# Two matmuls instead of three for a split product, with the correction sums in columns of their own

## The chip, the cores and the metric

The kernel runs on one core of a Trainium2 chip. The metric is the device time of one execution in microseconds. TensorE multiplies, VectorE and ScalarE work element by element and can read the accumulators (PSUM), GpSimd works on SBUF only, and SyncE sends most of the DMAs.

## The reference

Three stages, float32. A landmark attention (4 batches, 8 heads, 576 tokens, 64 per head, 32 landmarks) gives x of 2304 x 512. A first MLP follows, and then a second one, in which the change lies:

```
h = x @ w_in2                      # 2304 x 512 @ 512 x 2048
g = h * clip(h + 3, 0, 6) / 6
out = g @ w_out2                   # 2304 x 2048 @ 2048 x 512
```

## The kernel before

**Split numbers.** Float32 matrices are multiplied in a faster format (F32R) by splitting each operand into a high and a low part: `high = round(x)`, `low = x - high`. A product is then three passes, high x high, high x low and low x high (`PASSES`, line 21; the helper `passes`, line 132). The helper `split` (line 126) makes the parts of a tile: ScalarE casts the high one (line 128), VectorE subtracts to get the low one (line 129).

**Second MLP.** The 2304 tokens are worked off in three blocks of 768 (`i` = 0, 1, 2). In each block the first product of the MLP (`unit1`, eight units) fills `g`, 2048 x 768, in SBUF, and then the second (`product2`) multiplies it with w_out2. Both use a Strassen-like form with 7 products of quarter matrices instead of 8. The seven of the second product are called in the order `ORDER` = 0, 1, 6, 5, 4, 2, 3. Each takes a left factor of 384 tokens and a right factor of 256 columns and sums over `NU` = 8 steps `kp` of 128.

**One step** of `product2`: for four of the seven products VectorE first combines two quarters of `g` in place (lines 1021 to 1027, 128x384). `split` then makes the high and low part `s` of the left factor, 128x384 each, in a ring of 11 buffers, so that the splits can run that many steps ahead of TensorE. The right factors have been split long before and come from device memory as weight tiles `st` of 1 MB, half a product each, in six buffers. For each of `NQ` = 3 thirds `t` of 128 tokens TensorE does the three passes: a weight load (128 columns of `s`) and a matmul that moves 256 columns of `w`. The layout of `w` for one step is two column halves `j`, each with its high and low part `z` of 128 columns.

**Sums.** The three thirds accumulate in two PSUM banks of 512 columns, `qa` (thirds 0 and 1) and `qb` (third 2), from the pool `ps_o` of four banks, so that one product is summed while another is read. The pool `ps_h` (two banks) is used by `unit1` alone. After a product `evacuated` reads the sums: product 0 through ScalarE into `u2` (line 1048), the others through VectorE, which adds the running sums `u2`, `u3` (line 1050). Four of the seven products end in `stored`: the result goes to a tile `ob` and by a DMA of SyncE to the output (line 1058). Products 5 and 4 of the form are evacuated twice.

**Order of the work.** TensorE's and SyncE's instructions stand in the order in which the program writes them (`manual_schedule`); a planner with estimated durations orders those of VectorE, ScalarE and GpSimd and fills their gaps with later work. During a block's second product VectorE and ScalarE also make the next block's forms `yf` (`forms_y`, lines 917 and 129), from `yr`, which SyncE loads at the start of the block (`load_y`, line 905), behind the last output of the block before.

**GpSimd** has additions in `unit1` (lines 999 and 1002, 128x384) and, in the stages before, in the preparation of the weights (line 852, 128x128); in `product2` it has none.

Of the kernel before, what the change touches and what calls it, by code (L numbers as in the profile page):

```python
# [10 lines left out]
F32 = mybir.dt.float32  # L11
# [4 lines left out]
AF = mybir.ActivationFunctionType  # L16
ALU = mybir.AluOpType
# [3 lines left out]
PASSES = ((0, 0), (0, 1), (1, 0))  # L21
# [43 lines left out]
def kernel(  # L65
# [24 lines left out]
    nc = tc.nc  # L90
# [3 lines left out]
    P = 128  # L94
# [11 lines left out]
    scale = 1.0 / float(D) ** 0.5  # L106
# [16 lines left out]
    def pool(name, bufs=1, st=ctx, **kw):  # L123
        return st.enter_context(tc.tile_pool(name=name, bufs=bufs, reuse_waits="tile", **kw))

    def split(hi, lo, src, rest=nc.vector):
        return (
            nc.scalar.copy(hi, src),  # L128
            rest.tensor_tensor(out=lo, in0=src, in1=hi.bitcast(F32), op=ALU.subtract),  # L129
        )  # L130

    def passes(ps, lhs, rhs, first=True, last=True, **kw):
        for i, (x, y) in enumerate(PASSES):
            nc.tensor.matmul(ps, lhsT=lhs(x), rhs=rhs(y), start=first and i == 0, stop=last and i == 2, **kw)  # L134
# [27 lines left out]
    NU = NK // 2  # L162
# [548 lines left out]
    first = (mybir.EngineType.PE, mybir.EngineType.DVE, mybir.EngineType.Activation, mybir.EngineType.SP)  # L711
# [27 lines left out]
    ps_o = pool("ps_o", 4, space=PSUM)  # L739
    ps_h = pool("ps_h", 2, space=PSUM)  # L740
# [66 lines left out]
    NB, TB = 3, NT // 3  # L807
    TH, DH = TB // 2, DM // 2
    NQ = TH // P
# [146 lines left out]
    def ahead(i, z, j, h):  # L956
        stream(STREAM.index((i, z, j, h)) + NST)
# [54 lines left out]
    def product2(i, n_):  # L1012

        p = ORDER[n_]
        qa = ps_o.tile([P, 512], F32, tag="o", name="qa")
        qb = ps_o.tile([P, 512], F32, tag="o", name="qb")
        to = [qa[:, :DH], qa[:, DH:], qb[:, :DH]]
        for kp in range(NU):
            a11, a21, a12, a22 = (g[:, 2 * kp + f, TH * t:TH * (t + 1)] for f in range(2) for t in range(2))
            if p == 6:  # L1020
                nc.vector.tensor_tensor(out=a11, in0=a11, in1=a21, op=ALU.subtract)
            elif p == 5:
                nc.vector.tensor_tensor(out=a11, in0=a22, in1=a11, op=ALU.subtract)
            elif p == 4:
                nc.vector.tensor_tensor(out=a21, in0=a21, in1=a22, op=ALU.add)
            elif p == 2:
                nc.vector.tensor_tensor(out=a12, in0=a12, in1=a11, op=ALU.subtract)
            x = (a11, a12, a12, a22, a21, a11, a11)[p]
            pl, tag = shomes[ring[0] % len(shomes)]
            ring[0] += 1  # L1030
            s = pl.tile([P, 2, TH], F32R, tag=tag, name="s")
            split(s[:, 0], s[:, 1], x)
            if kp % 4 == 0:
                ahead(i, 1, n_, kp // 4)
                w = streams[i, 1, n_, kp // 4]
            for t in range(NQ):
                for m, (y, z) in enumerate(PASSES):
                    nc.tensor.matmul(  # L1038
                        to[t], lhsT=s[:, y, t * P:(t + 1) * P], rhs=w[:, kp % 4, :, z],
                        start=kp == 0 and m == 0 and t != 1, stop=kp == NU - 1 and m == 2,  # L1040
                        skip_group_check=t == 1,
                    )

        def evacuated(out, src, scale=1.0 / 6.0):
            for q_, cs in ((qa, slice(0, 512)), (qb, slice(512, TH // P * DH))):
                q_ = q_[:, :cs.stop - cs.start]
                if src is None:
                    nc.scalar.activation(out=out[:, cs], in_=q_, func=AF.Copy, scale=scale)
                else:
                    nc.vector.scalar_tensor_tensor(  # L1050
                        out=out[:, cs], in0=q_, scalar=scale, in1=src[:, cs], op0=ALU.mult, op1=ALU.add
                    )

        def stored(src, t, c, scale=1.0 / 6.0):
            ob = tp.tile([P, NQ * DH], F32, tag="ob", name="ob", bufs=2)
            evacuated(ob, src, scale)
            r0 = i * TB + t * TH
            nc.sync.dma_start(
                out=out[r0:r0 + TH, c * DH:(c + 1) * DH].rearrange("(t p) c -> p t c", p=P),
                in_=ob.rearrange("p (t c) -> p t c", t=NQ),  # L1060
            )

        if p == 0:
            sums[i] = [tp.tile([P, NQ * DH], F32, tag=f"u{x}", name=f"u{x}") for x in range(2)]
        u2, u3 = sums[i]
        if p == 0:
            evacuated(u2, None)
        elif p == 1:
            stored(u2, 0, 0)
        elif p == 6:  # L1070
            evacuated(u3, u2)
        elif p == 5:
            evacuated(u3, u3)
            evacuated(u2, u2)
        elif p == 4:
            stored(u3, 1, 1)
            evacuated(u2, u2)
        elif p == 2:
            stored(u2, 0, 1)
        else:  # L1080
            stored(u3, 1, 0, -1.0 / 6.0)
# [12 lines left out]
    with tc.manual_schedule(engines={mybir.EngineType.PE, mybir.EngineType.SP}):  # L1094
# [5 lines left out]
        for n, (x, kk) in enumerate(items):  # L1100
# [13 lines left out]
            if b == 0 and at_ in (NK + 4, NK + 6):  # L1114
                c = NC // 2 + (at_ - NK - 4) // 2
# [42 lines left out]
        tp = pool("tp", 1)  # L1158
# [8 lines left out]
        for i in range(NB):  # L1167
            if i + 1 < NB:
                load_y(i + 1)
            for u in range(NU):  # L1170
                unit1(i, u)
            later = Background(forms_y(i + 1)) if i + 1 < NB else Background()
            for n_ in range(7):
                product2(i, n_)
                later.step(1)
            later.finish()
# [32 lines left out]
```

## Time and profile before

| | |
|---|---|
| median of 3 runs | 816.11 us (815.37 to 816.56) |
| profiled execution | 816.88 us, span 815.1 us |
| TensorE matmul busy | 792.8 us (97%), 6146 matmuls |
| VectorE busy | 594.5 us (73%) |
| ScalarE busy | 464.7 us (57%) |
| GpSimd busy | 185.6 us (23%) |
| second product, blocks 0, 1, 2 | 511.8 to 572.4, 631.6 to 692.1, 750.4 to 811.1 us |

The span runs from the first to the last instruction of the profiled execution; the rest of its time lies around it. PE is TensorE, PEld its weight loads, DVE VectorE, ACT ScalarE, POOL GpSimd, SP SyncE; a q behind the name means the engine's instruction queue. Busy times of matmuls overlap, since the next begins before the last has drained.

### The profile page before, as it was taken

To read this page: it belongs to the slowest core of one execution; us is meant where nothing else is said; L and a number is where in the kernel's file an instruction comes from. 1 tells how busy PE (TensorE), PEld (TensorE's weight loads), DVE (VectorE), ACT (ScalarE), POOL (GpSimd) and SP (SyncE) were. 2 spreads that over 40 slices of the span, in tenths; PEclk is the share of its full clock that TensorE was granted. 3 is DMA by queue.
4 is the path that set the end of the run, shared out by engine and by line. 5 is a ranking of instruction groups with operands and counts; after the bars stand their busy time and mean duration, and the time that the engine had idled before them with its cause. 6 is when DMAs were issued, how large, how long until landed. Compare 5 with 4: busy or idle time off the path is not lost.

```text
span 815.1 us, 16385 instructions
## 1 busy us (share of the span) xinstructions
PE 792.8 (97%) x6146; PEld 739.4 (91%) x6146; DVE 594.5 (73%) x1215; ACT 464.7 (57%) x998; POOL 185.6 (23%) x275
## 2 busy tenths in 40 slices
PE   9788998999999999999999999999999999999997
PEld 6467787888988999988999999999999999999997
DVE  5778688768876778767795477994676994677962
ACT  4697556657665765666664455752455742555541
POOL 0000003244324433443660232000232000322000
PEclk9999999999999999999999999999999999999999
DMA  8998505587384973559655677777867677666751
GB/s 230 408 413 246 137 27 134 215 234 252 117 252 166 318 241 118 173 181 338 211 170 207 262 297 271 283 269 246 319 225 285 259 288 254 246 265 266 260 224 59
DMA packets 92559, 190.87 MB, mean 234 GB/s; under 512 B 39232, under 2 KB 66368, under 8 KB 85824
## 3 DMA queue, kind: packets, MB, share of 16 engines
q1 hardware_dynamic: 82944, 151.55, 53.4%
q0 software_dynamic: 9536, 38.28, 13.5%
q8 instruction: 48, 0.79, 0.4%
q14 instruction: 31, 0.25, 0.1%
HBM read 146.81 MB, written 42.99 MB: 233 GB/s over the span
## 4 chain that ended last, share of the span: by engine, by line
PE 85%; ACT 4%; DVE 4%; DMA 4%; issue 1%; SPq 1%; DVEq 0%; ACTq 0%
PE acc L134 20%; PE l L134 20%; PE qa L1038 15%; PE h L134 11%; PE qb L1038 7%; PE acc L793 2%; PE wp L683 2%; PE sa L433 2%; PE tp L276 1%; PE sc L347 1%; DMA raw<-in_moe_w_out_dram 1%; PE psr L517 1%; DMA raw<-in_moe_w_in_dram 1%; DMA yr<-y_d 1%; DMA w_d<-fa 1%
## 5 line engine op out<-in xcount | busy, mean ns | idle before, releaser
L134 PE MATMUL acc<-gs,wout 128*128 128x288 f32 (+1 forms) x1344 | 207.4, 300 | 0.0
L134 PEld LDWEIGHTS acc<-gs,wout 128*128 128x128 f32 x1344 | 186.1, 188 | 3.4 <-issue 1.5
L134 PE MATMUL l<-yf,st 128*128 128x384 f32 x1008 | 175.5, 335 | 0.7 <-DVE g L985 0.7
L134 PEld LDWEIGHTS l<-yf,st 128*128 128x128 f32 x1008 | 174.6, 188 | 1.0 <-DVE g L985 1.0
L1038 PE MATMUL qa<-st,s 128*128 128x256 f32 x1008 | 148.4, 283 | 0.0
L1038 PEld LDWEIGHTS qa<-st,s 128*128 128x128 f32 x1008 | 133.2, 192 | 0.0
L134 PE MATMUL h<-a,w 128*128 128x288 f32 (+2 forms) x768 | 129.4, 304 | 2.8 <-DVE gs L775 1.9
L128 ACT CAST s<-g 128x384 fp32r<-128x384 f32 x168 | 84.4, 512 | 80.5 <-PE qb L1038 54.2
L134 PEld LDWEIGHTS h<-a,w 128*128 128x128 f32 x768 | 108.4, 188 | 21.2 <-DVE gs L129 5.1
L129 DVE TENSOR_TENSOR s<-g,s 128x384 fp32r<-128x384 f32 x168 | 89.3, 560 | 20.4 <-ACT s L128 17.6
L852 POOL TENSOR_TENSOR raw<-raw 128x128 f32<-128x128 f32 x128 | 74.3, 592 | 76.0 <-DVE raw L865 41.2
L1038 PE MATMUL qb<-st,s 128*128 128x256 f32 x504 | 87.9, 283 | 0.0
L999 POOL TENSOR_TENSOR p<-p,p 128x384 f32<-128x384 f32 x24 | 26.3, 1095 | 237.9 <-ACT p L994 237.9
L774 ACT ACTIVATE t<-h 128x288 f32<-128x288 f32 (+2 forms) x120 | 49.5, 412 | 51.4 <-PE h L134 50.8
L775 DVE SCALAR_TENSOR_TENSOR t<-t,beta,h 128x288 f32<-128x288 f32 (+1 forms) x112 | 57.5, 513 | 28.2 <-ACT t L774 27.5
L1038 PEld LDWEIGHTS qb<-st,s 128*128 128x128 f32 x504 | 72.6, 192 | 0.0
L129 DVE TENSOR_TENSOR gs<-t,gs 128x288 fp32r<-128x288 f32 (+1 forms) x112 | 56.3, 503 | 18.3 <-ACT gs L128 17.9
L128 ACT CAST gs<-t 128x288 fp32r<-128x288 f32 (+1 forms) x112 | 49.0, 438 | 28.0 <-DVE t L775 26.4
L856 POOL DMA_DIRECT2D w_d<-fb x32 | 21.1, 661 | 77.0 <-DVE fb L129 47.6
L984 ACT ACTIVATE ta<-l,three 128x384 f32<-128x384 f32 x24 | 14.0, 583 | 38.5 <-PE l L134 38.5
L793 PE MATMUL acc<-gs,raw 128*128 128x256 f32 x128 | 31.8, 383 | 0.0
L990 ACT COPY p<-l 128x384 f32<-128x384 f32 x24 | 11.5, 479 | 34.5 <-PE l L134 34.5
(204 smaller groups left out, 1053.9 us busy)
## 6 DMA issues: line engine op xcount, KB each, us to landing
st<-w_d SPq DMA_DIRECT2D x48, 896.0 KB, 6.0
st<-w_d SPq DMA_DIRECT2D x42, 1024.0 KB, 5.5
w_d<-fb POOLq DMA_DIRECT2D x32, 512.0 KB, 4.2
w_d<-fa POOLq DMA_DIRECT2D x32, 384.0 KB, 3.2
raw<-in_moe_w_in_dram SPq DMA_DIRECT2D x16, 512.0 KB, 11.8
raw<-in_moe_w_out_dram SPq DMA_DIRECT2D x16, 512.0 KB, 11.5
raw<-in_moe_w_in_dram SPq DMA_DIRECT2D x64, 128.0 KB, 4.9
raw<-in_moe_w_out_dram SPq DMA_DIRECT2D x64, 128.0 KB, 4.8
```

The source lines that it names most:

```text
L128: nc.scalar.copy(hi, src),
L129: rest.tensor_tensor(out=lo, in0=src, in1=hi.bitcast(F32), op=ALU.subtract),
L134: nc.tensor.matmul(ps, lhsT=lhs(x), rhs=rhs(y), start=first and i == 0, stop=last and i == 2, **kw)
L433: nc.tensor.matmul(o[:, :, j], lhsT=qT[:, j, t * P:t * P + n], rhs=bdk[:, j], start=True, stop=True)
L683: nc.tensor.matmul(ps[g][js], lhsT=bd_t[b][gp, js], rhs=w[gp, j, cols], start=True, stop=True)
L774: nc.scalar.activation(out=t, in_=h, func=AF.Relu, scale=-1.0),
L775: nc.vector.scalar_tensor_tensor(out=gs[:, 0] if plain else t, in0=t, scalar=beta[:, kk:kk + 1], in1=h, op0=ALU.mult, op1=ALU.add),
L793: nc.tensor.matmul(acc, lhsT=words[kk][:, ms], rhs=gs[:, 0], start=at_ == 0, stop=at_ == NK - 1)
L852: nc.gpsimd.tensor_tensor(out=y[:, o], in0=p, in1=q_, op=op)
L856: nc.gpsimd.dma_start(out=to, in_=f.bitcast(F32))
L999: nc.gpsimd.tensor_tensor(out=p7, in0=p7, in1=p5, op=ALU.add)
L1038: nc.tensor.matmul(to[t], lhsT=s[:, y, t * P:(t + 1) * P], rhs=w[:, kp % 4, :, z], start=kp == 0 and m == 0 and t != 1, stop=kp == NU - 1 ...
```

## The change

For each step and third, two matmuls stand where three stood. The first loads the high part of the left factor and moves the high and the low half of the right factor side by side, 512 columns, into one whole PSUM bank: columns 0 to 255 collect high x high, columns 256 to 511 high x low. The second loads the low part and moves the high half, 256 columns, into columns 256 to 511. So each third has a bank of its own, three a product: in even calls all three from `ps_o`, in odd calls one from `ps_o` and two from `ps_h`. After a product ScalarE copies the three correction sums, scaled, to a tile `rest_` of 128x768 (under the tag `h2` of `unit1`); the main sums are evacuated as before, though in three pieces of 256; and GpSimd adds `rest_` to the result, before it is used or stored. The last product of the last block (`last`) keeps three passes into 256 columns and has no `rest_`.

```diff
-        qa = ps_o.tile([P, 512], F32, tag="o", name="qa")
-        qb = ps_o.tile([P, 512], F32, tag="o", name="qb")
-        to = [qa[:, :DH], qa[:, DH:], qb[:, :DH]]
+        last = i == NB - 1 and n_ == 6
+        homes = ((ps_o, "o"),) * 3 if n_ % 2 == 0 else ((ps_o, "o"), (ps_h, "h"), (ps_h, "h"))
+        to = [pl.tile([P, 2, DH], F32, tag=tag, name="q") for pl, tag in homes]
...
             for t in range(NQ):
-                for m, (y, z) in enumerate(PASSES):
-                    nc.tensor.matmul(
-                        to[t], lhsT=s[:, y, t * P:(t + 1) * P], rhs=w[:, kp % 4, :, z],
-                        start=kp == 0 and m == 0 and t != 1, stop=kp == NU - 1 and m == 2,
-                        skip_group_check=t == 1,
-                    )
+                high, low = (s[:, y, t * P:(t + 1) * P] for y in range(2))
+                first, final = kp == 0, kp == NU - 1
+                if last:
+                    passes(to[t][:, 0], lambda y: (high, low)[y], lambda z: w[:, kp % 4, :, z], first, final)
+                    continue
+                nc.tensor.matmul(
+                    to[t], lhsT=high, rhs=w[:, kp % 4].rearrange("p j z c -> p z j c"), start=first, stop=False,
+                    skip_group_check=True,
+                )
+                nc.tensor.matmul(
+                    to[t][:, 1], lhsT=low, rhs=w[:, kp % 4, :, 0], start=False, stop=final, skip_group_check=True
+                )

         def evacuated(out, src, scale=1.0 / 6.0):
-            for q_, cs in ((qa, slice(0, 512)), (qb, slice(512, TH // P * DH))):
-                q_ = q_[:, :cs.stop - cs.start]
+            for t in range(NQ):
+                cs = slice(t * DH, (t + 1) * DH)
                 if src is None:
-                    nc.scalar.activation(out=out[:, cs], in_=q_, func=AF.Copy, scale=scale)
+                    nc.scalar.activation(out=out[:, cs], in_=to[t][:, 0], func=AF.Copy, scale=scale)
                 else:
                     nc.vector.scalar_tensor_tensor(
-                        out=out[:, cs], in0=q_, scalar=scale, in1=src[:, cs], op0=ALU.mult, op1=ALU.add
+                        out=out[:, cs], in0=to[t][:, 0], scalar=scale, in1=src[:, cs], op0=ALU.mult, op1=ALU.add
                     )
+            if not last:
+                nc.gpsimd.tensor_tensor(out=out, in0=out, in1=rest_, op=ALU.add)
+
+        rest_ = tp.tile([P, NQ * DH], F32, tag="h2", name="qr")
+        for t in range(0 if last else NQ):
+            nc.scalar.activation(
+                out=rest_[:, t * DH:(t + 1) * DH], in_=to[t][:, 1], func=AF.Copy,
+                scale=(-1.0 if p == 3 else 1.0) / 6.0,
+            )
```

## Rows read from the trace of the kernel before

**Rows 1.** The page's part 1: busy us (share of span) x instructions.

```profile
PE 792.8 (97%) x6146; PEld 739.4 (91%) x6146; DVE 594.5 (73%) x1215; ACT 464.7 (57%) x998; POOL 185.6 (23%) x275
```

**Rows 2.** Windows of three stretches: length, busy PE PEld DVE ACT POOL, clock, DMA, GB/s.

```profile
511.80:572.40 60.60, 60.60 (x506) 60.60 (x505) 47.18 (x91) 29.34 (x56) 0.00 (x0) 1.00 0.74 270
631.60:692.10 60.50, 60.50 (x506) 60.50 (x506) 47.48 (x92) 29.27 (x57) 0.00 (x0) 1.00 0.74 269
750.40:811.10 60.70, 60.54 (x505) 60.34 (x503) 41.16 (x82) 25.07 (x49) 0.00 (x0) 1.00 0.53 193
```

**Rows 3.** Waits of TensorE, 500 to 815 us: total us, times, longest.

```profile
PE l L134 <- DVE g L985: 0.7, 1, 0.7
```

**Rows 4.** Chain of waits, 480 to 815 us: start, us, what (x matmuls).

```profile
514.27 0.72 PE qa L1038 x6
...
520.38 0.36 PE qb L1038 x3
...
692.23 58.24 PE l L134 x336
```

**Rows 5.** Chain of waits in the first MLP; these matmuls move 288 columns.

```profile
197.99 1.58 PE acc L134 x12
```

**Rows 6.** Tiles qa and qb: duration ns min/median/max, first and last start.

```profile
L1038 PE MATMUL qa<-st,s x1008: 278/283/284, 512.0 to 810.3; 128*128 128x256 f32 x168
...
L1050 DVE SCALAR_TENSOR_TENSOR ob<-qb,u x12: 414/416/428, 531.9 to 811.2; 128x256 f32<-128x256 f32 x12
...
L1048 ACT ACTIVATE u<-qb x3: 363/363/379, 520.9 to 759.3; 128x256 f32<-128x256 f32 x3
```

**Rows 7.** Timeline of VectorE, block 0: start, us, instruction, [idle before].

```profile
541.13 0.70 DVE L1050 SCALAR_TENSOR_TENSOR u<-qa,u 128x512 f32<-128x512 f32 x1
541.73 0.43 DVE L1050 SCALAR_TENSOR_TENSOR u<-qb,u 128x256 f32<-128x256 f32 x1
542.06 1.51 DVE L129 TENSOR_TENSOR s<-g,s 128x384 fp32r<-128x384 f32 x3
```

**Rows 8.** Lines 999 and 852 on GpSimd: duration ns min/median/max.

```profile
L999 POOL TENSOR_TENSOR p<-p,p x24: 1007/1015/1342, 457.6 to 747.0; 128x384 f32<-128x384 f32 x24
...
L852 POOL TENSOR_TENSOR raw<-raw x128: 399/518/1320, 123.5 to 425.5; 128x128 f32<-128x128 f32 x128
```

**Rows 9.** Timeline, first product of block 1: GpSimd beside VectorE.

```profile
583.65 1.01 POOL L999 TENSOR_TENSOR p<-p,p 128x384 f32<-128x384 f32 x1 [5.08 <-ACT p L994]
583.69 1.38 DVE L985 SCALAR_TENSOR_TENSOR g<-ta,h 128x384 f32<-128x384 f32 x1
...
585.69 1.19 POOL L1002 TENSOR_TENSOR h<-u,p 128x384 f32<-128x384 f32 x1 [1.03 <-DVE u L998]
586.04 1.25 DVE L1025 TENSOR_TENSOR g<-g 128x384 f32<-128x384 f32 x1
```

**Rows 10.** Windows, the slice of block 0's third product.

```profile
529.10:537.70 8.60, 8.60 (x74) 8.60 (x73) 8.60 (x19) 4.68 (x10) 0.00 (x0) 1.00 0.49 163
```

**Rows 11.** Timeline of VectorE, blocks 0, 1 and 2: three splits.

```profile
536.45 0.57 DVE L129 TENSOR_TENSOR s<-g,s 128x384 fp32r<-128x384 f32 x1
...
655.61 0.57 DVE L129 TENSOR_TENSOR s<-g,s 128x384 fp32r<-128x384 f32 x1
...
770.39 1.03 DVE L129 TENSOR_TENSOR s<-g,s 128x384 fp32r<-128x384 f32 x2
```

**Rows 12.** Timeline of SyncE's queue, start of block 1.

```profile
573.31 0.39 SPq L1058 DMA_DIRECT2D out_dram<-ob  x1
```

**Rows 13.** Chain of waits, 570 to 590 us.

```profile
573.92 7.14 DMA yr<-y_d
...
581.08 0.96 DVE t L917
```

**Rows 14.** Timeline of all engines at the end.

```profile
810.42 0.52 PE L1038 MATMUL qb<-st,s 128*128 128x256 f32 x3
...
811.23 0.41 DVE L1050 SCALAR_TENSOR_TENSOR ob<-qb,u 128x256 f32<-128x256 f32 x1
```

## The prediction

> **What bounds the kernel now.** Read first the page's busy line for TensorE [rows 1]: it is busy for 792.8 of 815.1 us, with as many weight loads as matmuls. Since matmuls overlap in the records, that alone proves nothing; the stretches do more. The change touches only the three stretches in which the second product of MLP2 runs, one for each third of the tokens (block 0, 1, 2). In each TensorE is busy from end to end and GpSimd does nothing, while VectorE is busy for 47 us of 60.6 in blocks 0 and 1 and for 41 us in block 2 [rows 2]. Next the waits: from 500 us to the end one wait of TensorE is listed, 0.7 us, and it is not in these stretches [rows 3]. So there the pace of TensorE is the time. The chain of waits gives that pace: six matmuls of 256 columns take 0.72 us and three 0.36 us, so each weight load with its matmul (a pair) takes 120 ns; with 384 columns 336 pairs take 58.24 us, 173.3 ns each [rows 4].
>
> **Matmuls.** Between those two widths 128 columns cost 53.3 ns, which is 0.417 ns a column, so 2.4 GHz, the clock granted in all three stretches [rows 2]; what is left of a pair is 120 - 106.7 = 13.3 ns, and 173.3 - 160 = 13.3 ns at the other width. Twelve pairs of 288 columns at 1.58 us leave 11.7 ns [rows 5]. A pair thus has a fixed part that doesn't grow with its columns. The change does for each (contraction step kp, token third t) two pairs of 512 and 256 columns where three of 256 stood: columns stay 768, one fixed part goes. There are 3 blocks x 7 products x 8 steps x 3 = 504 such groups; the very last product (24) keeps its three, so 480 x 13.3 ns = 6.4 us. No pair of 512 of this kind is in the trace, so both ends are open: 11.7 ns gives 5.6 us, and two fixed parts (the next load, too, fully hidden behind the long matmul) 12.8 us; nearest are the two rows that agree on 13.3. A step of 8 kp in a product is then 3 x 346.7 = 1.04 us where it was 1.08.
>
> The Trainium skill, "TensorE: Matmul & The Clock Gate", § Back-to-back issue gap, gives a lone matmul N/2.4 + 2.5 ns. By that only 2.5 ns would go per group, 1.2 us in all; the page itself says that pairs of load and matmul differ from it, and the 120 ns rows contradict it here by 10.8 ns a pair.
>
> **Evacuation.** A product's sum was read in two pieces, 512 and 256 columns; now in three of 256. On VectorE the two pieces start 0.60 us and 0.33 us apart [rows 7], so 0.93 becomes 1.0 us: 0.07 us for each of 8 evacuations of a block. ScalarE takes three copies of the correction columns, 0.36 us each at the row of that shape [rows 6], some 1.1 us a product: it has 31 us idle in the stretch [rows 2], and its casts run ten steps ahead, so I cost them at nothing; if that cover were gone, each product would lose 1.1 us, at most 22 us. Banks: the two halves of four become three of six, still one product being read while the next is summed.
>
> **GpSimd's adds.** Each evacuation but the last is followed by an addition of 128x768, nine in a block. The nearest rows are 128x384 at 1.01 us and 128x128 at 0.40 us at least [rows 8]: slope 2.4 ns a column, so 1.92 us (bounds 1.52, three times the 256 columns' 0.51 between, and 2.03, twice the 384). GpSimd has nothing else to do there, so the adds themselves are hidden. But look at what VectorE does beside GpSimd [rows 9]: an operation with both inputs in SBUF that takes 0.56 us elsewhere took 1.38 us when it started with GpSimd's at 583.7, and 1.25 us behind the one at 585.7. VectorE is held until GpSimd's instruction ends: 0.8 and 0.7 us lost of holds of 1.0 and 1.2. The subtraction of every split and every combination of g have both inputs in SBUF; evacuations, which read PSUM, do not. So an add of 1.92 us takes 1.4 to 1.7 us from VectorE; I take 1.5.
>
> The Trainium skill, "SBUF — State Buffer", § Who interferes with whom, says the same and more sharply: the port pair that VectorE and GpSimd share is an exclusive lock for the whole instruction. By the rule each add would cost the full 1.92 us, 1.7 us more over four adds, and the sum would be 814.6; the two stretched rows agree on the lock and show a little less of it, as VectorE finishes what it has begun.
>
> Where does this reach TensorE? In block 0 VectorE is busy in all of the third product's slice [rows 10], as it is from 511.8 to 546 us, since it also makes the next block's forms. The stretch has 56 steps of split, and step n starts on TensorE at 512.0 + 1.08 n [rows 6]. Counting the 29 splits that follow it back from the last, the split at 536.45 is that of step 26: done at 537.0, needed at 540.1, so 3.1 us early, the tightest of block 0. The split at 655.61 is step 25 of block 1: done at 656.2, needed at 631.7 + 27.0 = 658.7, 2.5 us early (30 follow). In block 2, where no forms are made, step 26's at 770.39 is 7.6 us early [rows 11]. Now TensorE comes 26 x 0.04 = 1.0 us sooner, one evacuation costs 0.07, and the adds of the first two products both precede the split: 3.0 us. Block 0: 3.1 - 1.0 - 0.1 - 3.0 = -1.0 us; block 1: -1.6; block 2: +3.5. So VectorE becomes the bound near steps 24 to 26 and 2.6 us of the gain go. Later margins in block 0 grow to 8 us by step 42, more than the three adds that come between (4.5). Bounds: 0 (the planner orders VectorE's work anew, and some combinations that stand before split 24 aren't needed until step 40) to 7 us (all five adds that come before step 42 at 1.92).
>
> **The store.** SyncE sends a product's output, then the next block's y, then weights, in order. At the end of block 0 the store went at 573.31, y at 573.92, it landed 7.14 us later, and VectorE's first use of it stood at 581.08, on the chain that ends in the 0.7 us wait of TensorE [rows 12, 13, 3]. Now the store waits for the add: ScalarE's copies and VectorE's pieces end 1.1 us behind the product, the add 1.9 us later, so y leaves some 2.4 us later in relation to TensorE. Behind VectorE's use of y queue the gates of the first product. If its place stays, 2.4 us are lost; if the planner moves it behind them, the 0.7 us may vanish. I take the middle, +0.8 us. The weight loads that wait behind the stores have six buffers of 4.2 us each and land in about 6, so 2 to 4 us later does them nothing.
>
> **End.** The last evacuation began at 811.23, behind the 0.69 us of the first, though TensorE ended at about 810.95 [rows 14]. As three pieces the first two are done while TensorE still runs: -0.2 us.
>
> **Sum.** -6.4 - 0.2 + 2.6 + 0.8 = -3.2 us. The profiled execution, 816.88 us (span 815.1 and 1.8 around it), becomes 813.7; it lies 0.8 above the median of the runs, so from 816.11 I forecast 812.9 us.
>
> **Rivals.** (a) The adds cost TensorE nothing: the order on VectorE is planned anew, the lead suffices, and y's move is hidden. For it: TensorE never waits in the stretches now. Against: 2.5 us of lead. 816.11 - 6.6 = 809.5.
> (b) Slower: VectorE doesn't make up for the holds. Place: the second to fifth products of blocks 0 and 1, with splits and evacuations late together, so that TensorE also waits for banks. The five adds before step 42 at 1.92 us and 0.35 us of evacuations against its margin of 8.1 less 1.7: 3.5 us a block, 7.0 in two, and y's use late by its whole 2.4 us: 816.11 - 6.6 + 7.0 + 2.4 = 818.9. It decides from 2.1 us of stall a block on (half of 6.6 less 2.4). For it: VectorE's full slices; against: it was idle for 13 us of each stretch, later on.
> (c) The change doesn't do what it says: a 512-column pair costs 240 ns, as two of 256, the fixed part belonging to columns. Against: the 384 row. With no gain, margins of 3.1 and 2.5 less 3.1 leave 0.6 us of stalls; 816.11 - 0.2 + 0.6 + 0.8 = 817.3, or 816 if y's delay is hidden.
> (d) The matmul page's rule: one pair less saves 2.5 ns a group, 1.2 us; stalls 0.7, y 0.8, end 0.2: 816.2. The 120 ns rows speak against it.
>
> **Chances.** Forecast 0.50 (its own range 810.3 to 815), (a) 0.22, (b) 0.12, (c) 0.08, (d) 0.08. A measurement of this kernel tells 0.2% (1.6 us, so below 814.5 or above 817.7) from no change. Faster: nine tenths of the forecast's 0.50 and all of (a), 0.67; slower: most of (b), and the upper ends of (c) and (d), 0.13; within 0.2%: 0.20. The range leaves out the best end of (a), (b) and part of (c): 809.2 to 816.4.
>
> **What would show it.** Right: steps of 1.04 us on TensorE; waits of TensorE for the split near steps 24 to 26 of blocks 0 and 1 and none in block 2; operations of VectorE stretched to 2 us beside GpSimd's adds of about 1.9 us. Wrong: a 512-column pair far from 226.7 ns, TensorE waiting for a bank, a wait of several us for the gates of block 1's first product, or no waits at all in the stretches.

## The result: slower, 820.5 us where 812.9 was forecast

The changed kernel took 820.53 us (median of 6 runs, 817.32 to 822.34) beside 815.74 us for the kernel before in the same comparison: ratio 1.0057, 95% interval 1.0035 to 1.0079. That is 4.8 us slower where 3.2 us faster was forecast, and above the range (809.2 to 816.4). Its profiled execution, 817.32 us (span 815.6), was the quickest of the six; a second profile of the same kernel, called changed_again below, took 820.62 us (span 818.9), which is the median of its own runs. Readings of the page are from the first profile, the mechanism from the second.

Part 1 of the page after, to be held against [rows 1]:

```profile
PE 788.4 (97%) x5666; PEld 713.5 (87%) x5666; DVE 617.1 (76%) x1239; ACT 477.6 (59%) x1061; POOL 269.4 (33%) x301
```

The 480 pairs are gone from TensorE (6146 to 5666 matmuls), VectorE is 23 us busier and GpSimd 84 us. Windows of the three second products after (columns as in [rows 2]):

```profile
510.30:571.40 61.10, 59.69 (x337) 51.27 (x337) 54.88 (x97) 32.20 (x75) 29.52 (x8) 1.00 0.60 223
633.10:694.70 61.60, 60.05 (x339) 51.43 (x338) 55.29 (x98) 32.41 (x77) 30.11 (x8) 1.00 0.62 224
752.90:811.60 58.70, 58.70 (x361) 52.60 (x360) 50.03 (x90) 29.55 (x68) 20.34 (x8) 1.00 0.53 200
```

Block 2 got the 2 us that the matmuls should give each block (60.7 to 58.7). Blocks 0 and 1 got longer instead, TensorE is idle there for 1.4 and 1.6 us, and VectorE's busy time rose by almost 8 us. GpSimd's eight adds show 29.5 us where eight of 1.9 us are 15. TensorE's waits after, from 450 us on, where [rows 3] had one of 0.7 us:

```profile
PE l L134 <- DVE g L985: 3.1, 1, 3.1
PE q L1046 <- DVE s L129: 2.5, 3, 1.4
```

Tiles after, with counts and durations min/median/max (the old ones are in [rows 6]): the new matmuls, the pieces of the evacuation, ScalarE's copies, and the adds.

```profile
L1042 PE MATMUL q<-st,s x480: 390/391/468, 510.3 to 802.5; 128*128 128x512 f32 x160
...
L1056 DVE SCALAR_TENSOR_TENSOR ob<-q,u x36: 404/410/426, 531.9 to 811.6; 128x256 f32<-128x256 f32 x36
L1064 ACT ACTIVATE qr<-q x60: 368/384/408, 518.8 to 803.0; 128x256 f32<-128x256 f32 x60
...
L1060 POOL TENSOR_TENSOR u<-u,qr x15: 1852/2164/11018, 520.6 to 800.0; 128x768 f32<-128x768 f32 x15
L1060 POOL TENSOR_TENSOR ob<-ob,qr x11: 1830/1839/6313, 533.1 to 805.6; 128x768 f32<-128x768 f32 x11
```

An undisturbed add takes 1.84 us (the median of those to `ob`), close to the 1.92 estimated; but the longest record is 11.0 us. What that is, is the heart of the case. The end (timeline of all engines) went as forecast: the three pieces began at 810.93, while TensorE still ran, and the store was issued at 812.10.

```profile
810.93 1.14 DVE L1056 SCALAR_TENSOR_TENSOR ob<-q,u 128x256 f32<-128x256 f32 x3 [5.45 <-PE q L134]
812.10 0.37 SPq L1073 DMA_DIRECT2D out_dram<-ob  x1
```

**Where the time went.** Start of block 0's first product, and the lengths of the stages behind it, read from TensorE's timelines, from the start of a stage's first matmul to the end of its last (us; block 0's first product is 58.4 in each):

| kernel | start | block 0, second | block 1, first | block 1, second | block 2, first | block 2, second |
|---|---|---|---|---|---|---|
| before | 453.71 | 60.62 | 59.35 | 60.63 | 58.40 | 60.62 |
| changed, first profile | 452.05 | 61.30 | 61.84 | 61.70 | 58.40 | 58.71 |
| changed_again | 451.99 | 61.17 | 65.27 | 61.74 | 58.44 | 58.71 |

The second profile less before: second products +0.55, +1.11 and -1.91; block 1's first product +5.92; the evacuation and store behind the last matmul -0.21 (4.16 us less 3.95); and all that precedes -1.7, where nothing was changed. No run explains that last term: block 0's first product starts at 453.71 in both profiles of a kernel with three matmuls, and at 451.6 to 453.3 in those with two. Sum +3.7, as the spans say (818.85 less 815.10). Against a second product without stalls, 58.40 us (below), the first two terms split into a gain of 2.22 each and stalls of 2.8 and 3.3.

### The profile page after: what moved, and what is told of

It is laid out like the page before. It is cut to its first block, busy times and chain, and to the rows that moved or that the text cites. A ratio compares the mean times of both kernels' runs of the same rounds, so it can differ in the third digit from the quotient of the medians.

```text
span 815.6 us, 15579 instructions
## 1 busy us (share of the span) xinstructions
PE 788.4 (97%) x5666; PEld 713.5 (87%) x5666; DVE 617.1 (76%) x1239; ACT 477.6 (59%) x1061; POOL 269.4 (33%) x301
## 3 DMA queue, kind: packets, MB, share of 16 engines
q0 software_dynamic: 9536, 38.28, 13.3%
## 5 line engine op out<-in xcount | busy, mean ns | idle before, releaser
L1042 PE MATMUL q<-st,s 128*128 128x512 f32 x480 | 167.9, 393 | 0.1
L1046 PE MATMUL q<-st,s 128*128 128x256 f32 x480 | 135.3, 282 | 2.9 <-DVE s L129 2.5
L129 DVE TENSOR_TENSOR s<-g,s 128x384 fp32r<-128x384 f32 x168 | 108.4, 683 | 3.5 <-ACT s L128 1.0
L1042 PEld LDWEIGHTS q<-st,s 128*128 128x128 f32 x480 | 89.9, 187 | 20.5 <-issue 0.7
L128 ACT CAST s<-g 128x384 fp32r<-128x384 f32 x168 | 80.3, 519 | 45.3 <-PE q L1046 22.6
L1046 PEld LDWEIGHTS q<-st,s 128*128 128x128 f32 x480 | 90.7, 189 | 5.3 <-DVE s L129 5.3
L1060 POOL TENSOR_TENSOR u<-u,qr 128x768 f32<-128x768 f32 x15 | 58.6, 3915 | 63.8 <-ACT u L1054 34.0
L1064 ACT ACTIVATE qr<-q 128x256 f32<-128x256 f32 x60 | 19.7, 383 | 52.6 <-POOL u L1060 41.0
L1060 POOL TENSOR_TENSOR ob<-ob,qr 128x768 f32<-128x768 f32 x11 | 25.2, 2293 | 40.1 <-DVE ob L1056 36.8
```

What stands on the lines that cost most here:

```text
L1042: nc.tensor.matmul(to[t], lhsT=high, rhs=w[:, kp % 4].rearrange("p j z c -> p z j c"), start=first, stop=False, skip_group_check=True,)
L1046: nc.tensor.matmul(to[t][:, 1], lhsT=low, rhs=w[:, kp % 4, :, 0], start=False, stop=final, skip_group_check=True)
L1060: nc.gpsimd.tensor_tensor(out=out, in0=out, in1=rest_, op=ALU.add)
L1064: nc.scalar.activation(out=rest_[:, t * DH:(t + 1) * DH], in_=to[t][:, 1], func=AF.Copy, scale=(-1.0 if p == 3 else 1.0) / 6.0,)
```

## The experiments

Theory A, formed from the first profile: the matmuls give their 6.4 us; GpSimd's adds give 6 us of them back, since an add and VectorE keep each other from running and ScalarE waits behind the add; and the store behind an add delays y, which costs block 1's first product the rest. Its rivals: new evacuations or banks cost it, VectorE has no room whoever adds, or the difference is elsewhere. All were timed beside the kernel before, in three groups of four; it took 815.65, 815.49 and 814.86 us in them.

**The same kernel again, with another profile.**

> The changed kernel as it is, for a second profile, since its profiled execution (817.3 us) was the fastest of six (median 820.5). Theory A (GpSimd's adds wait for VectorE and then hold it, ScalarE, SyncE's stores and the loads behind them wait for the adds): about 820 us, 4 to 5 us above the kernel before, with the same long GpSimd adds (10 us and more for the first product of blocks 0 and 1) and TensorE waiting 3 us or more in the second product of blocks 0 and 1, none in block 2, and 3 us or more for y. Rival B (a slower part elsewhere, before the second MLP): the same stalls as in the first profile, 6 us in two blocks, and the rest of the difference before 500 us.

Measured 820.62 us, 1.0063 [1.0045, 1.0081]. First the adds and VectorE, from the timelines of GpSimd, VectorE and ScalarE around block 0's third product (start, us, instruction, in brackets the idle time before and what ended it):

```profile
520.53 10.86 POOL L1060 TENSOR_TENSOR u<-u,qr 128x768 f32<-128x768 f32 x1 [11.25 <-ACT u L1054]
533.00 2.10 POOL L1060 TENSOR_TENSOR ob<-ob,qr 128x768 f32<-128x768 f32 x1 [1.62 <-DVE ob L1056]
```

```profile
528.19 1.49 DVE L1023 TENSOR_TENSOR g<-g 128x384 f32<-128x384 f32 x3
531.84 1.09 DVE L1056 SCALAR_TENSOR_TENSOR ob<-q,u 128x256 f32<-128x256 f32 x3 [2.16 <-ACT qr L1064]
532.84 0.55 DVE L1023 TENSOR_TENSOR g<-g 128x384 f32<-128x384 f32 x1
533.31 2.22 DVE L1027 TENSOR_TENSOR g<-g 128x384 f32<-128x384 f32 x1
```

```profile
531.42 0.94 ACT L1064 ACTIVATE qr<-q 128x256 f32<-128x256 f32 x3 [6.91 <-POOL u L1060]
532.23 3.00 ACT L128 CAST s<-g 128x384 fp32r<-128x384 f32 x7
```

Read them together. The add was ready at 520.53 and ended at 531.39. With its usual 1.85 us it began about 529.5, just as VectorE's unbroken run of operations came to its end (528.19 + 1.49 = 529.68): for 9 us VectorE did not let it in. VectorE stopped there because its next instruction, the evacuation of the second product (`ob<-q,u`), reads the running sum `u`, which this add was still writing. The wait that ended last was for the copies of L1064, 0.4 us behind the add: they want the only buffer `rest_`, which the add held, and ScalarE had stood still for 6.91 us, with seven casts for splits queued behind. So VectorE was idle for 2.16 us, behind an add that its own run of operations had kept out. The next add, ready when VectorE had just begun again, then held an operation of 0.55 us to 2.22. By 536.5 TensorE's split was late (waits of TensorE from 450 us on):

```profile
PE l L134 <- DVE g L985: 3.9, 1, 3.9
PE q L1046 <- DVE s L129: 2.3, 2, 1.4
```

The list shows only part of the loss. The starts of the 512-column matmuls show all pauses: 1.9 us in block 0 and 2.4 us in block 1 at steps 24 to 26, then 0.4 and 0.1 us at steps 31 and 29, then 0.3 and 0.6 us at the first step of the seventh product; the last 0.3 us of the 6.1 are a slower pace. The pauses at the seventh product are waits for banks, by their place: it takes the three banks of the fifth, and in block 1 each third begins just behind a piece of the fifth's late evacuation (VectorE and TensorE's weight loads; the piece ends at 689.93):

```profile
689.52 0.41 DVE L1056 SCALAR_TENSOR_TENSOR u<-q,u 128x256 f32<-128x256 f32 x1
690.04 0.19 PEld L1042 LDWEIGHTS q<-st,s 128*128 128x128 f32 x1 [0.36 <-issue]
```

Then y. SyncE's queue, and the chain of waits, of the same profile:

```profile
550.29 0.32 SPq L947 DMA_DIRECT2D st<-w_d  x1
565.00 0.39 SPq L1073 DMA_DIRECT2D out_dram<-ob  x1
565.49 1.85 SPq L947 DMA_DIRECT2D st<-w_d  x2
...
575.52 0.53 SPq L905 DMA_DIRECT2D yr<-y_d  x1
```

```profile
573.04 1.86 POOL ob L1060
574.91 0.39 SPq L1073
575.52 10.59 DMA yr<-y_d
586.13 0.96 DVE t L917
```

From 550.6 to 565.0 SyncE issued nothing: a store waited for its add, and the weight loads, in order behind it, came bunched. The last store waited until 574.91, y left at 575.52 (573.92 in [rows 13]) and now took 10.59 us instead of 7.14, beside those loads. That the loads made it longer is read from the trace and not tested by itself: in matmuls_alone (below), where no store waits for an add, it took 8.25. TensorE waited 3.92 us for the first gates. And after it, windows of TensorE (columns as in [rows 2]):

```profile
588.00:594.80 6.80, 4.92 (x15) 4.92 (x16) 5.21 (x10) 3.11 (x6) 1.18 (x1) 0.56 1.01 415
589.80:595.60 5.80, 5.72 (x18) 5.72 (x19) 3.96 (x9) 3.33 (x6) 0.42 (x1) 0.50 0.99 403
594.80:601.00 6.20, 6.20 (x35) 6.20 (x35) 3.80 (x8) 2.73 (x5) 2.03 (x2) 0.93 0.28 82
```

The granted clock stood at 0.56 in the stretch around the end of the wait, and at 0.50, so 1.2 of 2.4 GHz, from the first matmul behind it (589.88): the 18 matmuls of 384 columns there start 320 ns apart, but for the first and the last, and take 5.87 us where 18 of 173.3 ns would be 3.12, 2.7 us less. In the first profile the wait was 3.14 us, the clock stayed at 1.00, and the stage was 61.84 instead of 65.27 us: 3.4 us between two executions, 0.8 of the wait and the rest of the clock. The Trainium skill ("TensorE: Matmul & The Clock Gate", § What's actually happening) says that the lower clock is the default and that activity lifts it, so that an idle TensorE falls back; the trace agrees: behind 3.9 us of idle time the clock was 0.50, behind 3.1 us, in the other profile, 1.00.

**The matmuls alone.** GpSimd's adds and ScalarE's copies are left out, so the correction columns are summed and not used.

```diff
-            if not last:
-                nc.gpsimd.tensor_tensor(out=out, in0=out, in1=rest_, op=ALU.add)
-        rest_ = tp.tile([P, NQ * DH], F32, tag="h2", name="qr")
-        for t in range(0 if last else NQ):
...
```

> The two matmuls of the change, without the copies of the correction sums and without the adds (the correction terms are left out of the result). Theory A: TensorE's gain of 13.3 ns a group is whole, 480 x 13.3 ns = 6.4 us, and nothing stalls: 809.2 us (6.6 below the kernel before, within 1), each group at 346.7 ns in all three blocks. Rival C (the 512-column matmul itself costs more where DMA and VectorE are busy, as groups of 353 ns in blocks 0 and 1 suggest): 3 us less of gain, 812 to 813 us.

Measured 809.38 us, 0.9924 [0.9912, 0.9936], against 809.2 by A. Windows of the second products of blocks 0 and 1, and the 512-column matmuls:

```profile
510.30:568.70 58.40, 58.40 (x339) 51.51 (x338) 47.80 (x99) 29.07 (x57) 0.00 (x0) 1.00 0.79 279
628.90:687.30 58.40, 58.40 (x339) 51.55 (x338) 48.24 (x101) 28.76 (x57) 0.00 (x0) 1.00 0.78 279
```

```profile
L1042 PE MATMUL q<-st,s x480: 390/391/391, 510.3 to 794.7; 128*128 128x512 f32 x160
```

TensorE never waits there; 58.40 us is 168 groups of 346.7 ns (58.2) and the ends, as computed. So the matmul step, the evacuation in three pieces and the banks are right, and the loss is what the corrections need. Only block 1's first product is longer than before, 60.19 us with a wait of 1.5 us for the gates. Beside this window, VectorE's busy time in the changed kernel is 7 us longer in a block (54.88 against 47.80): that is how far eight adds stretch its operations, 0.9 us each on average; the time that it stands idle for an add comes on top.

**Two buffers for the copies.**

```diff
-        rest_ = tp.tile([P, NQ * DH], F32, tag="h2", name="qr")
+        rest_ = tp.tile([P, NQ * DH], F32, tag=("h2", "tb")[n_ % 2], name="qr")
```

> The changed kernel with the copies of the correction sums in two buffers in turn, so that ScalarE needn't wait for the last add before it copies the next product's sums. Theory A1 (ScalarE's wait for that one buffer, which keeps the casts of the splits behind it for 7 us, is what starves TensorE): 3 to 4 us below the changed kernel, about 817 us. Rival A2 (VectorE itself is the bound: held by the adds, and waiting in its own order for running sums that GpSimd hasn't finished): within 1 us of the changed kernel.

Measured 816.47 us, 1.0009 [0.9996, 1.0021]: 4 us of the loss are gone, the size expected, but not where (its profiled execution, 814.79 us, lies 1.7 below the median). The second products went from 61.17 and 61.74 to 60.41 and 61.06, 1.4 us together. Block 1's first product went from 65.27 to 60.44: y left at 574.64 and took 9.03 us, TensorE waited 1.8 us, and the clock stayed up. ScalarE's wait is about a quarter of the stalls. VectorE's idle time shrank only from 2.16 to 1.74 us, and now it is the add itself that ends it (VectorE's timeline):

```profile
531.89 1.09 DVE L1056 SCALAR_TENSOR_TENSOR ob<-q,u 128x256 f32<-128x256 f32 x3 [1.74 <-POOL u L1060]
```

**VectorE adds.** No GpSimd and no copies: VectorE adds the correction columns from PSUM, three more operations in each evacuation.

```diff
-            if not last:
-                nc.gpsimd.tensor_tensor(out=out, in0=out, in1=rest_, op=ALU.add)
...
+            for t in range(0 if last else NQ):
+                cs = slice(t * DH, (t + 1) * DH)
+                nc.vector.scalar_tensor_tensor(
+                    out=out[:, cs], in0=to[t][:, 1], scalar=scale, in1=out[:, cs], op0=ALU.mult, op1=ALU.add
+                )
```

> The correction sums added by VectorE straight from PSUM, three more pieces of 256 columns for each evacuation, no copies by ScalarE and no adds by GpSimd. Theory A (GpSimd's part is the cause, not the amount of work on VectorE): VectorE gets 1.0 us more for each of 9 evacuations of a block, at most 0.6 us of stalls near step 25 of block 1; y leaves 1.1 us later, at most 1.1 us: 810 to 811 us, 5 us below the kernel before. Rival D (VectorE simply has too little room, with or without GpSimd): 816 us or more, with waits of TensorE for the split in blocks 0 and 1.

Measured 815.46 us, 0.9996 [0.9985, 1.0006], so A's 810 to 811 missed, and D's 816 or more was nearly met. Without GpSimd the second products still take 60.57 and 61.12 us, with waits for banks and not, as D had it, for the split:

```profile
PE q L1042 <- DVE ob L1061: 2.0, 4, 0.7
PE l L134 <- DVE g L985: 1.1, 1, 1.1
PE q L1042 <- ACT s L128: 0.7, 1, 0.7
```

So it is not the lock alone: in this order of its work VectorE has no room for the corrections of all seven products in blocks 0 and 1, whether GpSimd holds it or it adds them itself (it is busy for 54.99 us of 60.5 here, with three more operations of 0.41 us in each evacuation).

**y early.** Block 2's y is fetched after the fourth product of the second MLP of block 0, when the forms are made and the buffer is free, and so on.

```diff
-            if i + 1 < NB:
-                load_y(i + 1)
+            if i == 0:
+                load_y(1)
...
+                if n_ == 3:
+                    later.finish()
+                    if i + 2 < NB:
+                        load_y(i + 2)
```

> The changed kernel with block 2's y loaded in the middle of block 0's second product (call 4 of 7), ahead of the stores that wait for GpSimd, instead of behind block 0's last store. Theory A (TensorE's wait of 3 to 4 us for the gates of block 1's first product comes from y, loaded late behind the store; where the wait is long enough TensorE's granted clock falls to 1.2 GHz for 6.8 us, which costs 3.4 us more): both go, block 1's first product takes 58 to 59 us instead of 61.8 to 65.3, and the kernel comes to 814 to 815 us; the second products keep their stalls, 61 us in blocks 0 and 1. Rival E (the wait comes from the backlog of VectorE, which GpSimd's adds leave behind): the wait stays, 819 us or more.

Measured 815.6 us, 1.0004 [0.9992, 1.0015], 5.0 us below the changed kernel, where A had 814 to 815. y is now issued at 542.89, and block 1's first product takes 58.44 us, without a wait. The second products keep their stalls, and block 0's grew by 1.7 us (62.85, 61.71). With the kernel before the same move gives nothing:

> The kernel before with nothing changed but the early load of block 2's y: a control for the last two. Both theories: its 0.7 us of wait goes, 0.5 to 1 us below the kernel before, about 814.8 us. If it were 2 us or more below, the gain of the other two would be y's and not the matmuls'.

Measured 815.22 us, 1.0003 [0.9995, 1.0012], where 0.5 to 1 us less was expected, though block 1's first product fell from 59.35 to 58.41.

**The forms later.** Every step of the next block's forms is put behind a product's evacuation, from the third product on, so that the first two have VectorE free; then the same with two buffers, and the same with VectorE adding.

```diff
...
-                later.step(1)
+                if n_ >= 2:
+                    with behind([ends[i, n_]]):
+                        later.step(2)
```

> The changed kernel with the next block's forms of y held back until the evacuation of the third call of the second product, so that VectorE makes them in the later calls, where it is idle, and block 2's first use of y no longer stands in block 1's first product. Theory A (the room on VectorE in calls 1 to 5, not its whole work, decides; block 2, which makes no forms, has no stalls): blocks 0 and 1 lose their stalls too, 58.4 to 59 us each, no wait for y: 809.5 to 811 us. Rival D (VectorE's whole work, with GpSimd's holds, is too much: 47 us, 1 us of evacuations, 9 holds of 1.5 to 1.9 us, in 58.4 us): stalls move to the later calls, 814 us or more.

> Forms held back and the copies of the correction sums in two buffers in turn. Theory A: the second buffer took 4 us off the changed kernel because ScalarE no longer waited for adds that VectorE's back-to-back stream kept waiting; with the forms held back there are gaps in that stream and the second buffer brings at most 1 us more: 809 to 810.5 us. Rival D: as with one buffer, 813 us or more.

> Forms held back and the correction sums added by VectorE from PSUM, without GpSimd. Theory A (what kept this form at 815.5 us was VectorE's backlog in the early calls, on which the banks waited): 56.7 us of VectorE's work in 58.4 us of a block, evenly spread, so 810 to 812 us. Rival D (VectorE's whole work decides): stalls remain, 814 us or more, and worse than with GpSimd's adds.

Measured 820.33 us (1.0052 [1.0036, 1.0069]), 816.14 (1.0007 [0.9996, 1.0017]) and 816.95 (1.0033 [1.0014, 1.0053]; its runs scatter from 815.56 to 821.94): A missed in all three, and the rival that the stalls move held. TensorE's waits in the first of them:

```profile
PE q L1046 <- DVE s L129: 7.7, 4, 2.9
PE l L134 <- DMA st<-w_d: 1.5, 1, 1.5
```

```profile
549.30 2.55 DVE L917 TENSOR_TENSOR yr<-yr 128x768 f32<-128x768 f32 x1
551.78 2.60 DVE L129 TENSOR_TENSOR yf<-yr,yf 128x768 fp32r<-128x768 f32 x1
```

The largest stalls now come from 549 us on (timeline of VectorE above): two of the forms' operations of 128x768, 0.96 us long elsewhere, stand beside two adds (549.19 to 553.57) and are stretched to 2.6 us, and ScalarE waited 4.1 us for one of them with casts queued behind. Second products: 62.84 and 62.81.

**Narrow adds.** The same add with the same waits, over 32 of its 768 columns; the other 736 are left without their corrections.

```diff
-                nc.gpsimd.tensor_tensor(out=out, in0=out, in1=rest_, op=ALU.add)
+                nc.gpsimd.tensor_tensor(out=out[:, :32], in0=out[:, :32], in1=rest_[:, :32], op=ALU.add)
```

> The changed kernel, but GpSimd adds only the first 32 of the 768 columns (the correction of the other columns is left out of the result): its instruction is short, its place in the chain is the same. Theory A (an add can't begin while VectorE runs one operation with two SBUF inputs into the next; the wait, not the add's own 1.85 us, makes the 10.9 us records): the first add of blocks 0 and 1 still stands for 8 us or more until VectorE stops, later adds and VectorE's stretched operations shrink by 1.6 us each; TensorE's stalls in blocks 0 and 1 shrink but don't go, y leaves some 1.6 us sooner and the clock stays up: 814 to 816 us. Rival F (GpSimd's own pace makes the long records): all adds under 1 us, no stalls, 810 to 811 us.

Measured 810.51 us, 0.9947 [0.9935, 0.996]. GpSimd's timeline, VectorE's operations at the end of the first record, and TensorE's waits:

```profile
520.03 10.34 POOL L1060 TENSOR_TENSOR u<-u,qr 128x32 f32<-128x32 f32 x1 [10.17 <-ACT u L1054]
531.33 0.25 POOL L1060 TENSOR_TENSOR ob<-ob,qr 128x32 f32<-128x32 f32 x1 [0.96 <-DVE ob L1056]
```

```profile
528.78 1.48 DVE L1023 TENSOR_TENSOR g<-g 128x384 f32<-128x384 f32 x3
```

```profile
PE l L134 <- DVE g L985: 0.8, 1, 0.8
```

This is the run that parts waiting from holding. An add whose own work is 0.25 us has a record of 10.34 us in the same place, and it ends at 530.37, 0.1 us behind VectorE's run (528.78 + 1.48 = 530.26): the long record is the wait for that run to break, as A said, and F's short adds fell. But A's 814 to 816 us missed, and the time is the one that F had: the second products are 58.40 us, free of stalls, although ScalarE waits 5.3 us for the add and VectorE 0.56 for the copies. The wait by itself costs TensorE nothing; the 1.85 us of access that each full add takes, by holding VectorE's operation (2.22 for 0.55) or by having VectorE idle until it ends (2.16 for 0.56), does.

**Two buffers and y early.**

> The changed kernel with two buffers for the copies and block 2's y loaded early. Theory A (two separate costs, which add): the second products of two_buffers (60.4, 61.1 and 58.7 us) with the first products of y_early (58.4 each): 812.5 to 814 us, 2 to 3 us below the kernel before. Rival G (both remove the same wait): as either of them alone, 815.5 us or more.

Measured 813.2 us, 0.9981 [0.9969, 0.9993], as A had it. Second products of 61.06 and 60.53 us, block 1's first product 58.41.

**The old form in the early products.** Two buffers, y early, and three passes as before in the first three products of blocks 0 and 1, while VectorE makes the forms.

```diff
-        last = i == NB - 1 and n_ == 6
+        last = n_ == 6 if i == NB - 1 else n_ < 3
...
```

> Two buffers, y early, and in blocks 0 and 1 the first three calls of the second product with three passes into 256 columns as before, without copies and adds; the other four calls and block 2 with the change. Theory A (VectorE has no room only in the early calls of blocks 0 and 1, where it also makes the forms): four calls x 24 groups x 13.3 ns = 1.3 us of gain in each of blocks 0 and 1 without stalls, 1.9 us in block 2, about 1 us from y, 0.2 us at the end: 809.5 to 811 us. Rival D (VectorE has no room in the later calls either, as when the forms were held back): blocks 0 and 1 stay at 60.6 us or more, 813 us or more.

Measured 811.32 us, 0.9957 [0.9945, 0.9969]: 3.5 us faster than the kernel before, and the best complete version here. From 450 us on not one wait of TensorE is listed. Window of block 0's second product, and TensorE's timeline in it:

```profile
511.50:571.40 59.90, 59.90 (x410) 55.41 (x410) 53.89 (x100) 32.46 (x68) 10.02 (x5) 1.00 0.75 280
```

```profile
537.40 0.40 PE L1042 MATMUL q<-st,s 128*128 128x512 f32 x1
537.64 0.28 PE L1046 MATMUL q<-st,s 128*128 128x256 f32 x1
537.75 0.40 PE L1042 MATMUL q<-st,s 128*128 128x512 f32 x1
```

A group starts every 353 ns here, not 346.7, and the product takes 59.99 us where 96 groups of 346.7 and 72 of 360 would make it 59.34; part of the groups behind the stalls of the changed kernel run at it, too. It costs 0.65 us in each of blocks 0 and 1, and the top of A's range (811) was missed by 0.3. What sets it is open.

## Why the prediction was wrong, step by step

- **Matmuls: right.** 13.3 ns a group was forecast, 6.4 us; the three second products without stalls (58.40, 58.40, 58.71) against 60.62, 60.63 and 60.62 give 6.35. The rivals by which 512 columns cost as two of 256, or 2.5 ns a group went, fell.
- **Evacuation and banks: right.** Three pieces take 1.09 us (1.0 forecast); no stall in the second products of matmuls_alone. The waits for banks in the changed kernel, 0.3 and 0.6 us, which the prediction named as a sign of being wrong, come from evacuations that VectorE does late, not from the number of banks.
- **GpSimd's adds: the step that failed.** "GpSimd has nothing else to do there, so the adds themselves are hidden", and "an add of 1.92 us takes 1.4 to 1.7 us from VectorE". The add (1.84 us) and the hold (1.67 of 1.85) were right for one add on a running VectorE; the exclusive lock that the Trainium skill states ("SBUF — State Buffer", § Who interferes with whom) is borne out in that direction. Overlooked was the other direction: VectorE's unbroken run keeps the add out, 9 us here, until VectorE itself needs what the add writes, and then VectorE stands idle for it. The prediction charged two adds of 1.5 us against one split's lead and had the margin recover; VectorE lost 3.8 us to them (2.16 idle, 1.67 held), and the stalls were 2.8 and 3.3 us, 6.1 instead of 2.6. The place forecast, steps 24 to 26, was right (4.3 of the 6.1 us, and none in block 2); but VectorE did not recover, and the other 1.8 us came behind it, where the prediction had none.
- **The store: mis-sized most.** "I take the middle, +0.8 us" became +5.9 (2.5 in the first profile). Its first half held: y left 1.6 us later, 2.8 in relation to TensorE, where 2.4 was forecast. What failed is "2 to 4 us later does them nothing" of the weight loads: the stores held them for up to 14.4 us, they came beside y, and y took 3.45 us longer. And no term stood for the clock behind such a wait of TensorE, 2.7 us in this profile; a wait of several us for the gates stood among the prediction's signs of being wrong.
- **End: right**, -0.2 forecast, -0.21 measured.
- **Sum.** Predicted -6.4 + 2.6 + 0.8 - 0.2 = -3.2. Measured -6.35 + 6.1 + 5.9 - 0.2 = +5.4, less the 1.7 before the stages, +3.7. So of the 6.9 us between the profiled execution forecast (813.7) and this one (820.62) the store's term has 5.1 and the adds' 3.5, less the 1.7. Rival (b) had the side, its stalls (7.0) and its time (818.9) nearly right, and its waits for banks came, though small; it was given 0.12 because the adds were counted against VectorE's idle time in the whole stretch, while the room was wanted in its first half, where [rows 10] already showed none. Two side sums of the prediction are off, and nothing rests on them: the lower bound of an add, 1.52 us, doesn't follow from [rows 8] (1.01 less 0.40 is 0.61 for 256 columns, not 0.51), and (c) with y's delay hidden is 816.5, not 816.

Shown by runs: the matmuls' gain (matmuls_alone, narrow_adds), the cost of the full adds (narrow_adds against changed_again), y's share (y_early), the lack of room on VectorE (dve_adds, old_early_calls). Only read from traces: that the clock made most of the difference between the two profiles of the changed kernel, that the bunched loads made y's flight longer, and that the pauses at the seventh product are waits for banks. Open: the pace of 353 ns, the 1.7 us ahead of the stages, and whether some order of the forms makes room for all seven products; the one tried did not.

## What to carry to other kernels

Work given to an idle GpSimd isn't free while VectorE runs unbroken operations on SBUF: count each such instruction on VectorE with up to its full length (1.67 us of 1.85 here), add the time that VectorE stands idle for its result, and ask in which stretch VectorE has that time, not how much it idles overall. When a store is made to wait for a later instruction, everything behind it in its queue waits as well; loads that others need soon should be issued ahead of it. A change that pays on one engine and charges another may be applied only where the other has room: here it stayed in 14 of 20 products, and with y fetched early 3.5 of 6.4 us stayed with it.

## What was not expected of the hardware

- An instruction of GpSimd that was ready at 520.0 recorded 10.34 us for 0.25 us of work: the record includes the wait for VectorE. Some 9 us of VectorE operations one behind the other did not let it in once.
- A wait of TensorE of 3.9 us was followed by a granted clock of 0.50, with 18 matmuls 320 ns apart instead of 173.3; one of 3.1 us, in another execution of the same kernel, left it at 1.00.
- The same two matmuls (512 and 256 columns) ran at 346.7 ns a group in all of matmuls_alone and narrow_adds, and at 353 ns on average behind products of three matmuls.
